# Loading v of batch 3 three issue slots earlier in a fused linear attention and SwiGLU kernel

## Chip, cores, metric

One core of one Trainium2 chip. The metric is the device time of one execution in microseconds (us), on that core. Every run is also listed with its span (first to last instruction) and the mean clock that was granted to TensorE; the span is about 1.8 us shorter than the time. "Full clock" below means a mean granted clock of 0.997 or higher in that list.

## The reference, cut to what matters

Eight batches of linear attention with eight heads (576 tokens, 64 dims a head), then one feed-forward layer over all 4608 tokens:

```python
q_p, k_p = phi(q), phi(k)              # relu, times cos and sin of the position
kv  = einsum('bhsf,bhsd->bhfd', k_p, v)  # per batch and head: 128 x 64
z   = sum(k_p, axis=2)
attn = (q_p @ kv) / (q_p @ z + 1e-6)
x   = rms_norm(attn as [4608, 512]) * rms_g
out = (silu(x @ w_gate) * (x @ w_val)) @ w_out
# ... float32 in and out; the kernel computes in bf16 with float32 sums
```

## The kernel before

The feed-forward work is a row of blocks: block `blk` has 12 steps (gate and value matmuls, 512 columns each) and 4 output steps, so 16 slots. The attention of the next batch is threaded into these slots: while block 2 runs, batch 3 is prepared (`b = nb - 1`). `at(blk, n, where, f, ...)` puts a piece of work into slot `n`; a slot number of 16 or more spills into the next block. All loads, stores and transposes that matter here are issued by one engine, SP, in program order.

```python
def load_kv(which, b, r0=0, r1=4, j0=0, j1=NJ):     # one piece: 288 KB
    ...
    return nc.sync.dma_start(out=raw[key][:, r0:r1, ...], in_=...)

def x_tr_dma(b, j):                                  # "x transpose j" below
    nc.sync.dma_start_transpose(out=x_dst(b, j), in_=xn_of[(b, j)][:, :])

def v_cast(eng, b, r0=0, r1=4, j0=0, j1=NJ):         # float32 v to bf16 vvm
    copy(eng, vvm[b % 2][:, r0:r1, j0:j1, 0:D], raw[("v", b)]...)

def kvz_mm(b, banks, rs=(0, 4)):                     # 72 small matmuls
    for r in range(*rs):
        for j in range(NJ):
            for c in range(2): nc.tensor.matmul(..., rhs=vvm[b % 2][lo:lo+64, r, j, :], ...)
# ... cut ...
for nb in range(2, B):
    b = nb - 1
    late = nb == 2
    vb, vn = (b, 3) if late else (b - 1, 14)
    if nb == 3:
        vb, vn = b, 1                                # batch 3: casts in block 2
    # ... cut ...
    for c in range(5):
        qn = (2, 3, 5, 5, 6)[c] if late else c       # batch 3: slot c of block 2
        at(b, qn, "post", q_phi, V, nb, c, 0)
        at(b, qn, "post", q_phi, A, nb, c, 1)
        at(b, qn, "post", q_tr_dma, nb, c)
    if not late:
        at(vb, vn, "post", v_cast, V, nb, *LOW)      # batch 3: slot 1
    at(vb, vn + 1 + (nb == 3), "post", v_cast, V, nb, *HIGH)   # batch 3: slot 3
    # key-value matmuls at slot 4 of block b; x transposes of batch 2: slots 8, 10, 12, 13 of block 1
    # ... cut ...
for nb in range(3, B):
    b = nb - 2
    for i, which in enumerate(("k", "v", "q")):
        for p in range(5 if which == "q" else 4):
            n = (0, 13, 6)[i] + p if b == 1 else 5 * i + p
            at(b + n // 16, n % 16, "post", load_piece, which, nb, p)

def gval_step(blk, n, bank=None):
    run(blk, n, "pe"); gval_mm(blk, n, bank); run(blk, n, "pre")
    sg = gval_act(blk, n, bank)
    gval_h(blk, n, bank, sg)                         # "gated product" on VectorE
    run(blk, n, "post")
```

The four pieces of v of batch 3 are called v0 to v3.

## Time and profile before

| | before |
|---|---|
| time, median of the first three runs | 328.99 us (328.81 to 329.25) |
| span of the profiled run, mean granted clock | 327.7 us, 0.997 |
| TensorE busy | 315.6 us, 96% |
| largest idle piece of TensorE after the opening | 1.67 us, block 2 |
| last x transpose of batch 2: issue, time to landing | 86.23 us, 2.4 us |

The page of the kernel before, its first table and its chain of waits:

```profile
span 327.7 us, 6406 instructions
PE 315.6 (96%) x2406; PEld 161.0 (49%) x2441; DVE 186.0 (57%) x412; ACT 176.7 (54%) x366; POOL 32.0 (10%) x67
...
PE 89%; DMA 4%; ACT 3%; DVE 2%; issue 1%; SPq 1%; ACTq 0%
```

TensorE is nearly always busy (96% of the span), so only its gaps are worth moving. The timeline of TensorE around the largest one (columns: start, duration, engine, source line, operation, output and inputs, count, and in brackets the idle time before and what ended it):

```profile
96.78 1.03 PE L426 MATMUL psV<-xnT,wv 128*128 128x512 bf16 x4
97.74 0.75 PE L282 MATMUL psA<-vvm,kpm 64*128 64x65 bf16 x36
100.16 0.72 PE L282 MATMUL psA<-vvm,kpm 64*128 64x65 bf16 x34 [1.67 <-DVE vvm L265]
```

Half of the 72 key-value matmuls of batch 3 run at 97.74; the other half waits for a cast on VectorE (`vvm`). The chain of waits (start, duration, what) says what that cast waited for:

```profile
94.74 0.71 SPq L246
95.45 0.05 issue
95.50 3.82 DMA rv<-in_v_dram
99.32 0.02 issue
99.34 0.77 DVE vvm L265
100.12 0.04 issue
100.16 0.75 PE psA L282 x36
```

Read upwards: the second half needs the cast (99.34), the cast needs v3, which was issued at 95.50 and took 3.82 us to land. The chain gives the cast's wait to the DMA, because that came last. How much later it came than the rest is in the timeline of VectorE:

```profile
97.91 0.69 DVE L441 TENSOR_TENSOR hT<-psV,sg 128x512 bf16<-128x512 f32 x1 [0.64 <-PE psV L426]
98.52 0.48 DVE L211 TENSOR_SCALAR qp<-rq,tab 128x512 bf16<-128x512 f32 x1
99.34 0.76 DVE L265 CAST vvm<-rv 128x1152 bf16<-128x1152 f32 x1 [0.34 <-DMA rv<-in_v_dram]
```

VectorE itself was busy up to 99.0, with a gated product and a q piece that stand ahead of the cast. It stood idle for v3 only 0.34 us. And the queue of SP, with the x transposes (L406), the stores (L456) and the v pieces (`rv`):

```profile
81.07 1.28 SPq L99 DMA_DIRECT2D rqt<-in_q_dram  x2
82.94 1.22 SPq L406 DMA_TRANSPOSE xnT<-xn  x1
84.26 0.53 SPq L456 DMA_DIRECT2D out_dram<-osb  x1
86.23 1.19 SPq L406 DMA_TRANSPOSE xnT<-xn  x1
87.54 0.50 SPq L456 DMA_DIRECT2D out_dram<-osb  x1
88.08 0.43 SPq L79 DMA_DIRECT2D rv<-in_v_dram  x1
...
95.50 0.57 SPq L79 DMA_DIRECT2D rv<-in_v_dram  x1
```

### The profile page before, as it was taken

To read this page: it belongs to the slowest core of one execution; us is meant where nothing else is said; L and a number is where in the kernel's file an instruction comes from. 1 tells how busy PE (TensorE), PEld (TensorE's weight loads), DVE (VectorE), ACT (ScalarE), POOL (GpSimd) and SP (SyncE) were. 2 spreads that over 40 slices of the span, in tenths; PEclk is the share of its full clock that TensorE was granted. 3 is DMA by queue.
4 is the path that set the end of the run, shared out by engine and by line. 5 is a ranking of instruction groups with operands and counts; after the bars stand their busy time and mean duration, and the time that the engine had idled before them with its cause. 6 is when DMAs were issued, how large, how long until landed. Compare 5 with 4: busy or idle time off the path is not lost.

```text
span 327.7 us, 6406 instructions
## 1 busy us (share of the span) xinstructions
PE 315.6 (96%) x2406; PEld 161.0 (49%) x2441; DVE 186.0 (57%) x412; ACT 176.7 (54%) x366; POOL 32.0 (10%) x67
## 2 busy tenths in 40 slices
PE   6899999999997999999999999999999999999994
PEld 2588465555444444544454445444544444444442
DVE  6875768777764765578257745773577133203310
ACT  6865775964774457645654576556644233223321
POOL 1660112001000100011001100110011000000000
PEclk9999999999999999999999999999999999999998
DMA  7999999898599566975597669956621400020014
GB/s 268 220 189 267 324 180 329 307 187 219 129 234 272 148 187 166 220 207 165 179 222 193 150 190 222 196 162 198 145 47 32 130 32 0 29 101 1 0 34 96
DMA packets 80337, 53.91 MB, mean 164 GB/s; under 512 B 51377, under 2 KB 67761, under 8 KB 80306
## 3 DMA queue, kind: packets, MB, share of 16 engines
q1 hardware_dynamic: 73264, 48.64, 57.2%
q0 software_dynamic: 6880, 4.72, 10.0%
q8 instruction: 19, 0.31, 0.4%
q10 hardware_dynamic: 162, 0.13, 0.1%
q14 instruction: 12, 0.10, 0.1%
HBM read 37.75 MB, written 9.44 MB: 144 GB/s over the span
## 4 chain that ended last, share of the span: by engine, by line
PE 89%; DMA 4%; ACT 3%; DVE 2%; issue 1%; SPq 1%; ACTq 0%
PE psC L446 26%; PE psG L426 25%; PE psV L426 25%; DMA rv<-in_v_dram 4%; PE psA L282 3%; PE psA L310 2%; PE psG L446 1%; PE psG L565 1%; PE psV L565 1%; PE psO L565 1%; ACT sg L435 1%; ACT kpm L209 1%; PE psC L830 1%; PE psV L254 1%; ACT qp L209 1%
## 5 line engine op out<-in xcount | busy, mean ns | idle before, releaser
L441 DVE TENSOR_TENSOR hT<-psV,sg 128x512 bf16<-128x512 f32 x102 | 70.3, 689 | 95.4 <-PE psV L426 70.6
L435 ACT ACTIVATE sg<-psG 128x512 f32<-128x512 f32 x102 | 60.7, 595 | 64.9 <-PE psG L426 63.4
L426 PE MATMUL psV<-xnT,wv 128*128 128x512 bf16 (+1 forms) x365 | 92.1, 374 | 0.4
L426 PE MATMUL psG<-xnT,wg 128*128 128x512 bf16 (+1 forms) x352 | 90.9, 374 | 0.7
L446 PE MATMUL psC<-wo,hT 128*128 128x512 bf16 x382 | 88.2, 379 | 0.7
L426 PEld LDWEIGHTS <-wv 128*128 128x128 bf16 x416 | 40.6, 98 | 47.4
L446 PEld LDWEIGHTS <-hT 128*128 128x128 bf16 x420 | 40.3, 98 | 46.7
L426 PEld LDWEIGHTS <-wg 128*128 128x128 bf16 x416 | 38.5, 98 | 41.0 <-DVE xnT L265 0.4
L263 ACT COPY osb<-psC 128x512 f32<-128x512 f32 (+1 forms) x33 | 19.2, 582 | 40.3 <-PE psC L446 38.9
L380 POOL TENSOR_TENSOR rs<-ms,mhalf 128x1 f32<-128x1 f32 x36 | 19.8, 551 | 201.1 <-ACT scr L375 201.1
L387 DVE SCALAR_TENSOR_TENSOR xn<-xt,rs,gb 128x512 bf16<-128x512 f32 x36 | 26.8, 745 | 17.1 <-POOL rs L380 17.1
L375 ACT ACTIVATE scr<-xt 128x513 bf16<-128x513 f32 x36 | 22.8, 635 | 22.9 <-DVE xt L364 22.7
L209 ACT ACTIVATE kpm<-rk,tab 128x256 bf16<-128x256 f32 (+1 forms) x78 | 32.0, 478 | 1.7 <-DMA rk<-in_k_dram 1.7
L364 DVE TENSOR_TENSOR xt<-psA,rec 128x512 f32<-128x512 f32 x35 | 24.2, 691 | 1.2
L211 DVE TENSOR_SCALAR kpm<-rk,tab 128x256 bf16<-128x256 f32 (+1 forms) x84 | 22.3, 329 | 2.2 <-DMA rk<-in_k_dram 2.2
L209 ACT ACTIVATE qp<-rq,tab 128x512 bf16<-128x512 f32 x32 | 22.4, 713 | 0.0
L211 DVE TENSOR_SCALAR qp<-rq,tab 128x512 bf16<-128x512 f32 x32 | 15.2, 489 | 0.1
L310 PEld LDWEIGHTS <-qpT 128*128 128x128 bf16 x248 | 11.6, 98 | 6.7 <-issue 0.3
L310 PE MATMUL psA<-kvzs,qpT 128*128 128x65 bf16 x248 | 12.8, 193 | 0.3
L282 PEld LDWEIGHTS <-kpm 64*128 64x128 bf16 x576 | 10.0, 94 | 5.6 <-issue 4.5
L426 PE MATMUL psG<-xnt_tail,wg 128*128 128x512 bf16 x48 | 12.3, 379 | 0.1
L282 PE MATMUL psA<-vvm,kpm 64*128 64x65 bf16 x540 | 10.6, 191 | 1.7 <-DVE vvm L265 1.7
(89 smaller groups left out, 168.6 us busy)
## 6 DMA issues: line engine op xcount, KB each, us to landing
out_dram<-osb SPq DMA_DIRECT2D x32, 256.0 KB, 2.5
rv<-in_v_dram SPq DMA_DIRECT2D x21, 288.0 KB, 3.2
rk<-in_k_dram SPq DMA_DIRECT2D x20, 288.0 KB, 3.9
rq<-in_q_dram SPq DMA_DIRECT2D x20, 256.0 KB, 3.2
rk<-in_k_dram SPq DMA_DIRECT2D x2, 1152.0 KB, 8.7
rq<-in_q_dram SPq DMA_DIRECT2D x2, 1024.0 KB, 8.5
rv<-in_v_dram SPq DMA_DIRECT2D x3, 576.0 KB, 8.1
wo<-in_moe_w_out_dram POOLq DMA_DIRECT2D x4, 384.0 KB, 7.2
```

What stands on the lines that cost most here:

```text
L209: nc.scalar.activation(out=out_ap, in_=in_ap, func=AF.Relu, scale=scale)
L211: eng.tensor_scalar(out=out_ap, in0=in_ap, scalar1=scale, scalar2=0.0, op0=ALU.mult, op1=ALU.max)
L282: nc.tensor.matmul(banks[c][:, r * E : (r + 1) * E], lhsT=kp_main[b][lo : lo + 64, j, r, :], rhs=vvm[b % 2][lo : lo + 64, r, j, :], start= ...
L310: nc.tensor.matmul(o[:, g, i, :], lhsT=qpT[(b, 0)][:, h, j * P : (j + 1) * P], rhs=kvz_of(b, h), start=True, stop=True,)
L364: nc.vector.tensor_tensor(out=xt[:, 0:DM].rearrange("p (b h d) -> p b h d", b=2, d=D), in0=o[:, :, :, 0:D], in1=rec[:, :, :].unsqueeze(3). ...
L375: nc.scalar.activation(out=scr[:, :], in_=xt[:, 0 : DM + 1], func=AF.Square, scale=1.0 / math.sqrt(DM), accum_out=ms[:, :],)
L380: nc.gpsimd.tensor_tensor(out=rs[:, :], in0=ms[:, :], in1=mhalf[:, :], op=ALU.pow)
L387: nc.vector.scalar_tensor_tensor(out=xn[:, :], in0=x_of[(b, j)][:, 0:DM], scalar=rs_of[(b, j)][:, :], in1=gb[:, :], op0=ALU.mult, op1=ALU. ...
L426: nc.tensor.matmul(pst[bank][:, cols[0] : cols[1]], lhsT=w[:, t, n * P : (n + 1) * P], rhs=x[:, t, cols[0] : cols[1]], start=(t == 0), sto ...
L435: nc.scalar.activation(out=sg[:, :], in_=psG[bank][:, :], func=AF.Silu)
L441: nc.vector.tensor_tensor(out=hTs[blk][:, n, :], in0=psV[bank][:, :], in1=sg[:, :], op=ALU.mult)
L446: nc.tensor.matmul(bank, lhsT=hTs[blk][:, n, j * P : (j + 1) * P], rhs=wo[:, n, :], start=(n == 0), stop=(n == NNT - 1),)
```

## The change

Its intent: v of batch 3 is loaded right behind q, so that the cast in block 2 need not wait for its last piece. All v pieces move three slots forward; no work is added or removed, and the order on the other four engines stays the same.

```diff
-                n = (0, 13, 6)[i] + p if b == 1 else 5 * i + p
+                n = (0, 10, 6)[i] + p if b == 1 else 5 * i + p
```

On SP this puts v0 and v1 around the q tails, v1 thus ahead of x transpose 2, v2 ahead of x transpose 3, the last of batch 2, and v3 behind the store that follows it.

## The prediction

> **What bounds the kernel.** TensorE: 315.6 of 327.7 us busy (96%, the engine table); the chain of waits gives it 89%. Outside the opening its biggest hole is in block 2: the timeline of TensorE has it idle 1.67 us before 100.16 us, between the two halves of the 72 key-value matmuls of batch 3. The chain of waits there: q transpose issue on SP 94.74, v load issued 95.50 (3.82 us to landing, 99.32), vvm cast on VectorE 99.34 (0.77), second 36 matmuls 100.16. That load is the fourth v piece of batch 3. SP issues in order, and this piece stands behind the x transpose into the tail tile (92.75) and the first q transpose of batch 3 (94.16), which waits for its q piece.
>
> **What the change does.** No work is added or removed. Four v issues move on SP from slots 13-16 to slots 10-13; the other engines keep their order. Laid out with the SP timeline's durations (0.5 to 0.6 us an issue, 1.2 a transpose): v0 81.1, v1 83.0, x transpose 2 at 83.6 (was 82.94), v2 85.4, x transpose 3 at 86.2 (unmoved: its operand is ready then), v3 about 88.1 instead of 95.50. The first three pieces took 4.2 to 4.9 us to land, so v3 lands near 92.5, 6.5 us ahead of need. The x transposes landed 2.4 to 2.9 us after issue, the last at 88.6; block 2 needs it at 90.74, so 2 us of slack covers more traffic (DMA share there 0.3 to 0.9). The q transposes of batch 3 and the k loads behind v3 come 0.6 to 1.7 us earlier; nothing waits for them.
>
> **How much is critical.** Little, because the DMA alone doesn't hold the cast. On VectorE, in order, the cast stands behind the gated product of step 3 (97.91, waits for that step's matmuls) and one q piece (98.52, 0.48). VectorE is free at 99.0 and waits only 0.34 us for the load. So the cast starts at 99.0 instead of 99.34, TensorE resumes at 99.8 instead of 100.16, and the hole shrinks from 1.67 to about 1.33 us; the rest is VectorE's order and stays. What follows is TensorE-bound (block 3: 35.16 busy of 35.32), so the 0.34 us should reach the end.
>
> [...] granted clock 1.00 across the hole.
>
> **Prediction.** 328.99 - 0.34 = 328.65 us; 328.3 to 329.1 holds it 8 times in 10 (the runs of before spread 0.44). Faster by over 2%: 0.005; within 2%: 0.99; slower by over 2%: 0.005.
>
> **What would show each step.** v3 issued near 88, landed before 94; the cast at about 99.0 without a DMA wait; the v load gone from the chain of waits at 95 to 99, VectorE (product, q piece, cast) in its place; hole about 1.3 us; block 2 still starting at 90.7.
>
> **What would make it wrong.** An x transpose of batch 2 landing after 90.7 [...]: TensorE would stall at the start of block 2 and lose the gain or more. Or the cast held by the DMA for more than the 0.34 us shown (a gain of up to 1.7 us). Or later waits absorbing the gain.

## The result, and the profile after

The time was 329.53 us, the median of six runs (329.06 to 330.44), against 329.21 us for six runs of before (328.81 to 329.32). The ratio of the two was 1.0014, with a 95% interval of 0.9997 to 1.0031: the same, and a median above the range that was predicted. (Ratios here are the mean time of one kernel's runs over that of the other's of the same rounds, so not quite the ratio of the medians that are quoted. Executions over 1.5% slower than the fastest of the same kernel are left out of the means.) The six runs fell into two groups: 329.06, 329.09 and 329.18, and 329.89, 329.92 and 330.44. The profiled one is the longest. What it shows first is that SP issued v as laid out:

```profile
83.38 0.60 SPq L79 DMA_DIRECT2D rv<-in_v_dram  x1
84.08 1.23 SPq L406 DMA_TRANSPOSE xnT<-xn  x1
85.41 0.53 SPq L456 DMA_DIRECT2D out_dram<-osb  x1
86.00 0.41 SPq L79 DMA_DIRECT2D rv<-in_v_dram  x1
86.52 1.20 SPq L406 DMA_TRANSPOSE xnT<-xn  x1
87.82 0.51 SPq L456 DMA_DIRECT2D out_dram<-osb  x1
88.79 0.33 SPq L79 DMA_DIRECT2D rv<-in_v_dram  x1
```

v3 went out at 88.79 and took 4.4 us to land, so at 93.2. The timeline of VectorE has the cast behind the q piece without a wait in brackets:

```profile
99.33 0.69 DVE L441 TENSOR_TENSOR hT<-psV,sg 128x512 bf16<-128x512 f32 x1 [0.64 <-PE psV L426]
99.94 0.48 DVE L211 TENSOR_SCALAR qp<-rq,tab 128x512 bf16<-128x512 f32 x1
100.33 0.76 DVE L265 CAST vvm<-rv 128x1152 bf16<-128x1152 f32 x1
```

But TensorE has a new hole, ahead of the old one:

```profile
90.75 0.38 PE L446 MATMUL psC<-wo,hT 128*128 128x512 bf16 x1
92.16 1.02 PE L426 MATMUL psG<-xnT,wg 128*128 128x512 bf16 x4 [1.02 <-DMA xnT<-xn]
...
101.14 0.75 PE L282 MATMUL psA<-vvm,kpm 64*128 64x65 bf16 x36 [1.23 <-DVE vvm L265]
```

The old hole fell from 1.67 to 1.23 us. The new one, 1.02 us at the first step of block 2, waits for x transpose 3. That transpose took 5.6 us to land, which the chain of waits shows as one piece:

```profile
85.69 0.75 DVE xn L387
86.44 0.08 DVE kpm L211
86.52 5.60 DMA xnT<-xn
92.12 0.04 issue
92.16 1.02 PE psG L426 x4
```

In the profile of before the same transpose landed 2.4 us after its issue. So one profile offers a simple story: v2 ahead of the transpose makes it late, and TensorE loses more than it gained. The experiments had to say whether that is the rule or one run.

To compare profiles, each span is cut at two events of TensorE: the first key-value matmul of batch 2 (in block 1) and the first of batch 4 (in block 3). That makes three parts: the opening, which comes before anything that the change moves; the stretch, which holds everything that it moves; and the rest. The rest was 194.15 to 194.24 us in all 20 profiles. The stretch of before was 66.47 us (133.50 - 67.03), that of this profile 67.21 (134.48 - 67.27).

### The profile page after: what moved, and what is told of

Read it like the earlier page. It is cut to its first block, busy times and chain, and to the rows that moved or that the text cites. A ratio compares the mean times of both kernels' runs of the same rounds, so it can differ in the third digit from the quotient of the medians.

```text
span 328.7 us, 6404 instructions
## 1 busy us (share of the span) xinstructions
PE 316.7 (96%) x2406; PEld 160.9 (49%) x2441; DVE 185.8 (57%) x412; ACT 176.7 (54%) x366; POOL 32.1 (10%) x67
## 4 chain that ended last, share of the span: by engine, by line
PE 80%; DMA 8%; DVE 4%; ACT 4%; issue 2%; POOL 1%; ACTq 0%; SPq 0%; DVEq 0%
PE psV L426 24%; PE psG L426 24%; PE psC L446 23%; DMA wv<-in_moe_w_val_dram 4%; PE psA L282 3%; PE psA L310 2%; DMA xnT<-xn 2%; PE psG L446 1%; ACT kpm L209 1%; DMA rk<-in_k_dram 1%; DMA rv<-in_v_dram 1%; DVE xt L364 1%; ACT sg L435 1%; ACT scr L375 1%; PE psV L254 1%
## 5 line engine op out<-in xcount | busy, mean ns | idle before, releaser
L426 PE MATMUL psV<-xnt_tail,wv 128*128 128x512 bf16 x47 | 12.1, 379 | 0.0
```

The source lines that it names most:

```text
L426: nc.tensor.matmul(pst[bank][:, cols[0] : cols[1]], lhsT=w[:, t, n * P : (n + 1) * P], rhs=x[:, t, cols[0] : cols[1]], start=(t == 0), sto ...
```

## The experiments

Four theories are named in the expectations: Q, a v piece issued directly ahead of x transpose 3 delays its landing; N, the late landing was chance; L, the total traffic of the stretch delays it; A, what is issued after it does. O says that the rest of the hole is the order of work on VectorE, and its rival P that it is not. All kernels gave correct results. In the diffs, the slot of a v piece is given by a table.

### 1. The changed kernel again

No edit.

> The changed kernel once more, for the spread: its six runs fell near 329.1 (three) and near 329.9 (three, one of them the profiled one at 330.44). Theory Q (a v piece issued directly ahead of the x transpose 3 makes that transpose land late, TensorE stalls about 1.0 us at the start of block 2): runs between 329.0 and 330.4, mean 0.2 to 0.6 us above before, the profile shows transpose 3 landing 4 us or more after issue, and the stall is as long as that landing is late. Rival N (the 1.02 us stall of the one profile was a chance event of that run): transpose 3 lands in under 3.5 us, no stall, mean 0.3 us below before.

Measured: 329.98 us median (328.79 to 330.3), ratio 1.0006 (0.9983 to 1.0030). Transpose 3 landed 4.0 us after issue, later than the 2.4 of before, but in time: no wait at the start of block 2, hole 1.23 us, stretch 66.03 us. So the stretch was 0.44 us shorter than before, and yet the span was 328.3: the opening took 68.06 us against 67.03. Neither theory met all its numbers. The delay of Q is there; the stall isn't the rule.

### 2. v2 and v3 behind the last x transpose

```diff
-  n = (0, 13, 6)[i] + p if b == 1 else 5 * i + p
+  n = (p, (10, 11, 13, 14)[p % 4], 6 + p)[i] if b == 1 else 5 * i + p
```

> v pieces 0 and 1 early as in the change, pieces 2 and 3 in slots 13 and 14, behind x transpose 3. Theory Q: transpose 3 lands 2.4 to 3.5 us after issue, no stall at the start of block 2 (TensorE goes from the output matmuls of block 1 to block 2 without a gap), v3 still lands before 96, hole between the key-value halves about 1.25 us; time 0.3 to 0.5 us below before, 0.6 to 0.9 below the changed kernel. Rival L (it is the total traffic of the stretch, v0 and v1 included, that slows the transposes): transpose 3 still lands 4.5 us or more after issue and part of the stall stays.

Measured: 328.62 us median (328.48 to 330.42), ratio 0.9983 (0.9959 to 1.0007). Transpose 3 landed 2.4 us after issue, stretch 66.02, hole 1.23. L is out: v0 and v1 were as early as in the change, and the transpose was as quick as before.

### 3. All pieces one slot earlier, v0 directly ahead of transpose 3

The same edit with `(12, 13, 14, 15)`.

> All v pieces one slot earlier than before (12 to 15): one v piece, v0, stands directly ahead of x transpose 3, nothing else of v is early; v3 goes ahead of the tail x transpose instead of behind the first q transpose. Theory Q: transpose 3 lands 4.5 to 5.6 us after issue, stall of 0 to 1 us at the start of block 2 although only one piece moved ahead; time 0 to 0.6 us above before. Rival L: with only one piece more in the stretch the landing is under 3.5 us and the time is 0.3 us below before.

Measured: 328.96 us median (328.47 to 329.85), ratio 0.9984 (0.9962 to 1.0005), no stall, stretch 66.05. The views give no landing of transpose 3 in this run, but the kept trace has its signals (see "All profiles side by side"): the last came at 90.72 us, 4.5 us after issue, and block 2 began at 90.76, just in time. That is within what Q expected, but mostly by one late signal: the other fifteen were there after 2.9 us. One slot was as good as three for the hole.

### 4. v3 back in its old place

The same edit with `(10, 11, 12, 16)`.

> As the change for v0 to v2, but v3 back in slot 16, behind the first q transpose as before. Theory Q: the same late x transpose 3 (4.5 to 5.6 us) and stall as the change, and the v3 wait of before on top (hole about 1.5 us): time 0.3 to 0.5 above the changed kernel. Rival A (it is what is issued after transpose 3, the store and v3 at 88.8, that slows it [...]): transpose 3 lands under 3.5 us and no stall.

Measured: 328.88 us median (328.80 to 331.57), ratio 0.9996 (0.9967 to 1.0025). Transpose 3 landed in 3.3 us, stretch 66.03, hole 1.23: a miss. I had expected the old wait for v3. With the other pieces out of the way SP issued v3 28.22 us after the start of the stretch (95.10 - 66.88) instead of 28.47 (95.50 - 67.03), and the cast was no longer held. The wait for v3 was that marginal. With v3 gone from behind the transpose it landed in 3.3 us, against 3.4 to 5.6 in the change. By the numbers (under 3.5 us, no stall) this is the outcome of A, and Q's 4.5 to 5.6 us did not come. But 3.3 us is still 0.9 us more than the 2.4 of before: v2 alone delays the transpose, and v3 behind it may add a little.

### 5. to 7. The second cast moved ahead on VectorE, with three placements of v

```diff
-  at(vb, vn + 1 + (nb == 3), "post", v_cast, V, nb, *HIGH)
+  at(vb, vn + 1, "post", v_cast, V, nb, *HIGH)
```

The cast goes from the end of step 3 of block 2 to the end of step 2, ahead of the gated product of step 3. With v at slots 10, 11, 13, 14:

> v pieces at slots 10, 11, 13, 14 as in the run with v2 and v3 behind x transpose 3, and the second v cast of batch 3 moved on VectorE from the end of step 3 to the end of step 2 of block 2, ahead of the gated product of step 3. Theory O (the 1.23 us hole that is left with v early is the order on VectorE: product of step 3, q piece, then cast): the hole disappears, and the stretch from the start of the key-value matmuls of batch 2 to the second half of those of batch 3 falls from 32.7 to about 31.4 us (33.13 before); time about 1.7 us (0.5%) below before. Rival P (the hole is made by something else, psA or the wait itself): stretch stays at 32.7.

With v as in the change:

> The change itself with the same move of the cast. Theory O: no hole, stretch 31.4 us, plus whatever x transpose 3 costs at the start of block 2 in this run (0 to 1.2 us); mean time 1.3 to 1.7 us below before. If the late transpose is rare, within 0.3 us of the run with v2 and v3 behind it; if it is the rule, 0.5 to 1 us worse than that.

With v as before:

> The v loads as before, only the cast moved to step 2. Theory O with the v load as the other holder: the cast stands waiting for v3 (landing about 99.3), the product of step 3 and its q piece wait behind it, TensorE resumes at about 100.2 as before: stretch 33.0 to 33.2, hole about 1.6, time within 0.3 us of before. That is: neither move alone pays more than 0.45 us, both together pay 1.7. Rival: the cast's order alone is what counts: stretch falls to 32 or less.

Measured, with the stretch and the hole of each profile:

| v pieces | cast | median us | mean of full-clock runs | stretch | hole |
|---|---|---|---|---|---|
| before | step 3 | 330.02 | 329.25 (6 of 11) | 66.21 to 66.71 (3 profiles, all rounds) | 1.41 to 1.91 |
| before | step 2 | 329.13 | 329.02 (5 of 6) | 66.38 | 1.58 |
| the change | step 2 | 327.70 | 328.04 (5 of 6) | 64.62 | none |
| 10, 11, 13, 14 | step 2 | 327.37 | 327.50 (6 of 6) | 64.63 | none |

The ratios were 0.9959 (0.9918 to 1.0000), 0.9930 (0.9884 to 0.9976) and 0.9905 (0.9866 to 0.9944). Five of the eleven runs of before were below full clock in these rounds and long, which makes the ratios too good; the full-clock means say 1.75 us for the best. Its TensorE timeline has all 72 matmuls in one piece:

```profile
96.57 1.03 PE L426 MATMUL psV<-xnT,wv 128*128 128x512 bf16 x4
97.53 1.33 PE L282 MATMUL psA<-vvm,kpm 64*128 64x65 bf16 x72
```

O is shown: the 1.23 us that an early v left was VectorE's order. And neither move pays much alone. With the cast at step 2 but v as before, VectorE stands waiting at the head of its queue, as this line of its timeline shows:

```profile
98.79 0.77 DVE L265 CAST vvm<-rv 128x1152 bf16<-128x1152 f32 x1 [1.98 <-DMA rv<-in_v_dram]
```

Against the first profile of before, the move of the load gave 0.44 us of stretch, that of the cast 0.09 (66.47 - 66.38, inside before's own spread), and both together 1.84 (66.47 - 64.63).

### 8. The suspected cost doubled

The edit with `(10, 11, 12, 12)`: v2 and v3 directly ahead of transpose 3.

> The suspected cost doubled: v2 and v3 both issued directly ahead of x transpose 3 (slots 10, 11, 12, 12). Theory Q (a v piece directly ahead delays the landing of the transpose): transpose 3 is issued about 0.5 us later and lands 5 to 8 us after issue, in every profile late enough for a stall of 1 to 3 us at the start of block 2; stretch 33.7 to 35.5 us, time 0.6 to 2.3 us above before. Rival N (the late landing of one profile was chance with no tie to the v pieces): landing 2.4 to 4 us, no stall, stretch 32.7.

Measured: 329.84 us median (328.73 to 333.77; three of six runs below full clock), ratio 0.9986 (0.9930 to 1.0042). Transpose 3 was issued at 86.66 and landed 4.0 us later; block 2 began 0.26 us late, and the stretch was 66.28. So the sign was that of Q, but the size was far below what I had expected, and one run could not rule out N.

### 9. to 12. One more look at before, three at the change

> The kernel before, a second profile of it. If the spread of run times lies in the opening: the start of the key-value matmuls of batch 2 falls anywhere from 66.5 to 68.1 us, while the stretch from there to those of batch 4 is 66.47 us again (within 0.1) and the rest to the end is unchanged; transpose 3 lands 2.4 to 2.5 us after issue. Rival: the stretch of before itself moves by some tenths from run to run.

> The changed kernel, a third profile. Theory Q with chance on top: transpose 3 lands 3.3 to 5.6 us after issue; below about 4 us no stall and the stretch from the key-value matmuls of batch 2 to those of batch 4 is 66.03 us; above it the stretch grows by as much as the landing is late (67.2 at 5.6). Rival N: landing near 2.5 in most profiles.

> The changed kernel, a fourth profile: as the third. Stretch 66.0 (no stall) in two of three profiles, 66.2 to 67.3 in one.

> The changed kernel, a fifth profile: as the third. Stretch 66.0 (no stall) in two of three profiles, 66.2 to 67.3 in one.

Measured: 329.41 us for before, 328.69, 328.81 and 329.19 for the change, one run each at full clock. The stretch of before was 66.71. It moved by 0.24 from the first profile, as the rival had it, so my "within 0.1" was wrong. The wait for v3 is a race with VectorE and varies: the hole was 1.41 to 1.91 us in the three profiles of before. The three of the change had 66.02, 66.02 and 66.03, with transpose 3 landing in 3.9, 3.9 and 4.0 us and no stall.

### 13. to 16. The rate of the stall and the noise of a comparison

Two more of the change, one more of the kernel of experiment 2, and before run as if it were a kernel to be tested.

> The changed kernel, sixth profile, with times. The stretch from the key-value matmuls of batch 2 to those of batch 4 is 66.03 us when x transpose 3 lands within about 4 us of issue (4 of 5 profiles so far) and up to 1.2 us longer when it lands later (1 of 5). If a late landing is common (one run in three), the mean of the changed kernel equals that of before; if rare (one in ten), it lies 0.3 to 0.5 us below.

> The changed kernel, seventh profile, with times: as the sixth. [...] the others lie within 326.5 and 328.3 us of span.

> v2 and v3 behind x transpose 3, second profile, with times: transpose 3 lands in 2.4 to 2.5 us as before, no stall, stretch 66.03; mean of its runs 0.3 to 0.6 us below before and at or below the changed kernel, its slowest run at good clock faster than the slowest of the changed kernel if late landings matter.

> The kernel before, third profile, as a kernel of its own, with times: stretch 66.4 to 66.8; transpose 3 lands in 2.4 to 2.5 us; its six runs against the runs of before in the same rounds give the noise of such a comparison: ratio within 0.3% of 1 with an interval of about 0.3%, which is as wide as the effect that is looked for.

Measured, on one chip:

| kernel | median us | ratio, 95% | stretch | transpose 3 |
|---|---|---|---|---|
| the change | 329.99 | 1.0003 (0.9975 to 1.0030) | 66.03 | 3.9 |
| the change | 329.37 | 0.9993 (0.9967 to 1.0019) | 66.02 | 3.8 |
| v2 and v3 behind | 328.80 | 0.9969 (0.9944 to 0.9993) | 66.03 | 2.9 |
| before, against itself | 330.39 | 1.0020 (0.9988 to 1.0052) | 66.21 | 2.4 |

The last row is the most useful one: the kernel before came out 0.2% slower than itself, with an interval of 0.64% in width. An effect of 0.44 us is 0.13%.

### 17. and 18. The dose raised to four, and a last look at the change

All four pieces in slot 12, directly ahead of transpose 3:

```diff
+  n = (p, 12, 6 + p)[i] if b == 1 else 5 * i + p
```

> The dose raised: all four v pieces (1.18 MB) in slot 12, directly ahead of x transpose 3, none of them elsewhere. Theory Q (what is issued directly ahead of the transpose delays its landing): issue at about 87.2 instead of 86.2 and landing 4 to 7 us later, at 91.5 to 94, so a stall of 1 to 3 us at the start of block 2 in the profile, named as a wait for the transpose; stretch 67 to 69 us against 66.0 without a stall; mean of the runs at full clock 0.5 to 2.5 us above before. Rival N (the late landing is chance with no tie to v): landing 2.4 to 4 us, no stall, stretch 66.0.

> The changed kernel, eighth profile, with times. Late landings in 1 of 7 profiles so far, and 8 of 23 runs at full clock with a span of 328.1 us or more (none of 11 with v2 and v3 behind the transpose): one to three of these six runs again at 328.1 or more at a clock of 0.997 or higher, and the lowest near 327.0.

Measured for four pieces: 332.72 us median (331.49 to 334.2), ratio 1.0100 (1.0066 to 1.0134), slower, with an interval clear of 1, and its three full-clock runs lay within 331.49 and 331.84. Stretch 68.42. The lines of SP's queue and of TensorE:

```profile
84.91 1.86 SPq L79 DMA_DIRECT2D rv<-in_v_dram  x4
86.87 1.20 SPq L406 DMA_TRANSPOSE xnT<-xn  x1
```

```profile
89.71 1.24 PE L446 MATMUL psC<-wo,hT 128*128 128x512 bf16 x5
93.18 1.04 PE L426 MATMUL psG<-xnT,wg 128*128 128x512 bf16 x4 [2.23 <-DMA xnT<-xn]
```

Landing after 6.3 us, issue 0.6 later, stall 2.23 us: as Q expected. N, which denies any tie to v, falls; whether chance adds to the delay of Q is the question of the next section. The last look at the change: 328.90 us median (328.66 to 330.00), ratio 0.9982 (0.9957 to 1.0007), stretch 66.02, landing 3.4 us, one of six full-clock runs at 328.2 us of span.

### All profiles side by side

| v pieces issued directly ahead of x transpose 3 | time to landing, us | block 2 late by |
|---|---|---|
| none (before 3, before with the cast at step 2, v2 and v3 behind 2, the same with the cast at step 2) | 2.4 (5 times), 2.5, 2.9 | 0 |
| v2 (the change, 8 profiles) | 3.4, 3.8, 3.9 (3 times), 4.0 (2 times), 5.6 | 0 in seven, 1.2 in one |
| v2 (two other kernels: v3 late, cast at step 2) | 3.3, 3.8 | 0 |
| v0 (experiment 3, from the signals below) | 4.5 | 0.03 |
| v2 and v3 | 4.0 | 0.26 |
| v0 to v3 | 6.3 | 2.4 |

("Late by" is how much longer than 30.70 us it took from the start of the stretch to the key-value matmuls of block 2; that is a little more than the idle time in brackets.)

The kept traces hold more than these views show. A landing is counted in 16 signals, and the time to landing is that of the last one. Read one by one from the packed traces of the runs, the signals say:

- **What the transpose follows.** In all 13 profiles with v directly ahead, the fifteenth signal of transpose 3 came 0.51 to 0.64 us after the last signal of the v piece just ahead of it, whether that piece took 3.3 us to land (experiment 3) or 6.2 (the fourth of four pieces). With two pieces ahead, v3 took 3.9 us, about as long as v2 in the change (3.5 to 4.0), so two cost no more than one.
- **What the stalled profile had besides.** Fifteen of its 16 signals were there at 90.64 us, 4.1 us after issue, and block 2 could have started on time (about 90.98, an estimate: 90.74 plus the 0.24 by which this opening was longer). The last came at 92.12, 1.48 us behind the fifteenth. In the other seven profiles of the change that distance was at most 0.07 us. Experiment 3 had such a straggler too, 1.63 us behind, with the fifteenth signal at 2.9 us.
- **Stragglers are not peculiar to the change.** In the first profile of before, 11 of the 145 transfers of SP whose signals can be told apart had the last one more than 0.8 us behind the fifteenth.

So Q and chance share the stall: in the change v2 costs the transpose 0.9 to 1.7 us in every profile (fifteenth signal, less 2.4), and in one a straggler came on top. The margin that was left in the other seven was 0.15 to 0.7 us (an estimate: the start of block 2 in before, moved by the difference of the openings, less the last signal).

The transposes next to it bear Q out and limit it. X transpose 2 landed in 3.5 to 4.9 us in the 14 profiles with v1 directly ahead, and in 2.4 to 2.5 in the five with no v in its way (3.7 in experiment 3, with a straggler). X transpose 1 has a q piece of 256 KB directly ahead in every kernel and landed in 2.8 to 3.0. It too came right behind that load (fifteenth signal 0.59 us after the load's last in the first profile of before, 0.66 in that of the change), but there the load landed 3.0 us after its issue, and its cost was small (2.8 to 3.0 us, where x transpose 2 with no v in its way took 2.4 to 2.5).

And the opening, which no kernel here touches, took from 66.54 to 68.06 us in the 20 profiles. The two longest, 68.06 both, are two runs of the change (experiment 1 and the first of 13 to 16) in which the granted clock sank to half in the opening (0.50 from 10 to 12 us); the other 18 lay within 66.54 and 67.44. The stretch from 8 to 14 us, as busy time and count of PE, PEld, DVE, ACT and POOL, then the granted clock, the DMA share and GB/s; first the change in experiment 1:

```profile
8.00:14.00 6.00, 5.94 (x98) 4.05 (x96) 4.30 (x13) 4.17 (x11) 3.93 (x6) 0.72 1.12 276
```

and before:

```profile
8.00:14.00 6.00, 5.29 (x106) 3.33 (x105) 4.98 (x15) 5.26 (x15) 3.29 (x5) 1.00 0.99 251
```

The loss is 6 us times 0.28, or 1.7 us of clock; at the 0.50 that both runs show from 10 to 12 us, such a dip is about 3.4 us long (an estimate: 1.7 over the half that is lost). In both runs it began at about 9 us (an estimate: the granted clock was 1.00 up to 8 us, then 0.81 and 0.77 from 8 to 10), and from 14 us on it was 1.00 again. Why a given run loses it, no run here shows.

The run times split accordingly:

| | full-clock runs | mean | range | of them 329.9 or more | runs below full clock |
|---|---|---|---|---|---|
| before (listed with a clock) | 27 | 329.26 | 328.62 to 330.02 | 2 | 15, mean 331.18 |
| the change | 29 | 329.45 | 328.66 to 330.69 | 9 | 4, mean 329.98 |
| v2 and v3 behind | 11 | 328.76 | 328.48 to 329.45 | 0 | 1, 330.42 |

These pool several chips and rounds. The kernel with v2 and v3 behind the transpose lies 0.50 us below before, close to the 0.44 of its stretch. The change has the same stretch without a stall, and its lower runs are near those, but a third of its full-clock runs are 329.9 or longer. Of its six profiled full-clock runs one was that long, and that is the one with the stall. That the other eight long ones stalled too is likely but argued: they have no profile kept.

## Why the prediction was wrong

Point by point, in the order of the prediction:

- **What bounds the kernel, and the hole.** Right: TensorE, and the 1.67 us hole with v3 and VectorE at its edge.
- **The order on SP.** Right to within 0.7 us: v3 was issued at 88.79 and landed at 93.2 (predicted 88.1 and 92.5).
- **The cast starts at about 99.0 without a wait, and the hole falls to 1.33 us.** Right: the wait was gone in every profile of the change, and the hole was 1.23 or 1.24 us in all eight. The gain in the stretch was 0.44 us against the profile of before that I read (0.19 to 0.69 against its three profiles), where 0.34 was predicted. That the rest of the hole is VectorE's order was shown by moving the cast.
- **"2 us of slack covers more traffic".** This step failed. It costed the slack with landing times of 2.4 to 2.9 us, measured with no v piece directly ahead of transpose 3. With v2 there it took 3.3 to 5.6 us: 0.9 to 1.6 us of the 2 us were gone in nine of ten profiles (landing less 2.4 us), and in the tenth all of it. The delay alone never used up the slack: the one stall (1.02 us idle, 1.19 in the stretch) took the delay, 1.7 us at the fifteenth signal, and a straggler of 1.48 us. The prediction named the danger and gave neither a time in the sum. Queue order as the reason of the delay is the author's guess. What the runs show is that SP issued v2 and the transpose one behind the other (86.00 and 86.52), that the landing grew with the pieces ahead (none, one, four: 2.4 to 2.9, 3.3 to 5.6, 6.3 us), and that the transpose's fifteenth signal followed the last of the piece ahead by 0.51 to 0.64 us each time. They show arrivals, not what a DMA engine was doing in between.
- **"What follows is TensorE-bound, so the 0.34 us should reach the end".** Right: the rest was 194.15 to 194.24 us everywhere.
- **"328.3 to 329.1 holds it 8 times in 10 (the runs of before spread 0.44)".** This term of the sum was mis-sized, and it decided. Three runs spread by 0.44 us; the 27 full-clock runs of before spread by 1.40, and 15 of its 42 runs, below full clock, averaged 331.18. In the profiles the opening varied most, by 0.9 us at full clock and by 1.5 with the two of lower clock; the stretch of before varied by 0.5 and the rest of the span by 0.09. (No profile of before below full clock was kept, so where those runs lost their time is not shown.) Before's full-clock runs, moved down by the 0.34, would reach from 328.28 to 329.68. The measured median, 329.53, has three of its six runs in the upper group: one stalled (the profile), one at a clock of 0.993, and one at full clock without a profile. Without the one stall that was seen it would be about 329.2 (an estimate: 330.44 less 1.19 in the list of six), still above 329.1: so the range failed by the spread, not by the stall alone.

So the mechanism of the gain was right and its size nearly so; the loss beside it was thought covered and was not always; and both are smaller than the run-to-run spread of a part of the kernel that I had not looked at.

What stays open: why one of 16 signals comes 1.5 us late in some transfers; whether the long full-clock runs of the change are all stalls; and why a run loses the clock in the opening.

The version that beats both kernels has v at slots 10, 11, 13, 14 and the second cast at step 2: 327.37 us median (327.18 to 328.29), 1.75 us below before at full clock.

## What to carry to other kernels

When a profile puts a wait down to a load, read on the waiting engine's own timeline how long it stood idle for it: here 0.34 of 1.67 us, and the load and the order of the waiting engine had to be moved together to get all of it. An earlier load also stands ahead of something else that the same engine issues: check what stands right behind its new place, and re-cost that one's landing with a load ahead of it (here 3.3 to 5.6 us instead of 2.4 to 2.9), and with some margin, since the last of its 16 signals can straggle (here by 1.48 us in one of eight profiles of the change). And before promising a range of tenths, compare several runs of the unchanged kernel, and cut profiles at landmarks, so that a noisy opening (here 66.54 to 68.06 us) doesn't drown what a change does in its own stretch.
